# Sigmoid attention with a squared-ReLU feed-forward layer: another order of products in 48 units, and other idle products at the start

## The chip, the core and the metric

The kernel runs on one core of a Trainium2 chip. The metric is the device time of one execution in microseconds (us). A core has five engines with queues of their own: TensorE (PE, with its weight loads shown apart as PEld) multiplies, VectorE (DVE) and ScalarE (ACT) work element by element, GpSimd (POOL) does nearly nothing here, and SyncE (SP) issues the transfers.

## What is computed

The first part is an attention whose softmax is replaced by a sigmoid, over 8 batches of 12 heads, 448 positions and 64 numbers a head. Its result, 3584 tokens of 768 numbers, goes through a feed-forward layer with a hidden width of 2048:

```python
scores = q @ k.T / sqrt(64) - log(448)
x = sigmoid(scores) @ v              # 3584 tokens x 768
h = x @ w_in                         # 768 -> 2048
g = s * relu(h) ** 2 + b
out = g @ w_out                      # 2048 -> 768
```

All inputs and outputs are float32.

## The kernel before

**Attention (lines 352 to 406).** A loop goes over 24 groups of four heads. For each group `scores` and `scores_last` make the scores with float32 products over half the rows (64 of 128 partitions), two at a time; ScalarE takes the sigmoid of each pair of banks (line 354), `attn_v` and `attn_v_last` multiply by v, and the result goes to memory. The tiles of the sigmoids have eight buffers (the pool `ap_`, tag "a"). In the same steps VectorE and ScalarE convert the weights, which come as 64-bit numbers, and form sums of blocks of them (the planner of lines 416 to 469), which are stored for later.

**The start.** The first group's queries and keys are loaded in two halves, `load(..., first=True)`, lines 344 and 345: k, q, k, q. Meanwhile TensorE runs `WARM` = 17 idle products of a tile of zeros in bfloat16 (lines 410 to 412), 256 columns each, into a PSUM tile `idle` that nobody reads. Then come the scores of the first group: six pairs for the first half of the queries, and six for the second.

**Feed-forward layer.** Each float32 matrix is split into a high part, rounded to float32r, and a low part, the rest. A product of two matrices is made of three: high x high, high x low and low x high (`PARTS`, line 37: index of the weights' part, index of the tokens' part). The first 512 tokens are computed plainly: line 487 (`ffn1`) puts 18 products into one bank, line 666 (`ffn2`) three into each of six banks. The other six blocks of 512 tokens are computed three at a time, in two rounds (`n` = 0 and 1), with a scheme that takes 15 block products instead of 18, for either layer.

**The units of the first layer.** A round has 60 units, 15 block products `i` by four parts `p` of the hidden width, in the order of `L1` (line 554), which is written out by hand in `CHAINS_1`: the block products of a chain go to the same PSUM tile `bk`, of two banks, and the parts of a pair (0, 1) or (2, 3) take turns. A unit is twelve products of 128x128 weights with 512 columns: for each of its two banks `j`, two blocks `c` of the inner dimension, and for each the three of `PARTS`. So its first six products go to bank 0 and the next six to bank 1, and the second product of each three has the same weights as the first (line 922, inside three loops):

```python
for j in range(2):
    m = 0
    for c in range(KC):
        for wi, xi in PARTS:
            nc.tensor.matmul(bk[:, j], wt[:, j, wi, c * P : (c + 1) * P], opd[i][xi][:, c, :], ...)
```

After each unit `results_1` (lines 795 to 838) copies or adds `bk`, both banks in one instruction, into tiles in SBUF on ScalarE or VectorE; `square` and `scale` follow. The weights `wt` of a unit come by one transfer of 512 KB into one of seven buffers, which the SP queue issues six units ahead (`fetch`). Other jobs for the operands of later units (`first_jobs`) are placed in the units by hand (`places`). The second layer, line 1049, has 60 units of twelve products as well, each half of which adds to a bank.

Of the kernel before, what the change touches and what calls it, by code (L numbers as in the profile page):

```python
# [12 lines left out]
F32R = mybir.dt.float32r  # L13
# [4 lines left out]
AF = mybir.ActivationFunctionType  # L18
# [16 lines left out]


TB = 512
WARM = 17
PARTS = ((0, 0), (0, 1), (1, 0))
AHEAD = 6  # L40
PIECES = (2, 1, 1, 2, 1, 1, 2, 1, 1, 2, 1, 1, 2, 1, 1, 2, 1, 1, 2, 1, 2, 1)
# [43 lines left out]
def sigmoid_attention_relu2_ffn(  # L85
# [11 lines left out]
    nc = tc.nc  # L97
    B, NQ, P, _, S = q.shape
    D = v.shape[5]
    NF, _, DM = w_in.shape  # L100
# [4 lines left out]
    KC = NCC // 3  # L105
# [8 lines left out]
    def pool(stack, name, bufs, side=None, space=None):  # L114
        kw = dict(side=side) if side else {}
        if space is not None:
            kw["space"] = space
        return stack.enter_context(
            tc.tile_pool(name=name, bufs=bufs, reuse_waits="tile", **kw)
        )  # L120
# [22 lines left out]
    first = ExitStack()  # L143
# [11 lines left out]
    zero = const.tile([P, 2 * P], BF16, name="zero")  # L155
# [170 lines left out]
    ap_ = pool(at, "ap", 8)  # L326
# [7 lines left out]
    half = (slice(0, D), slice(D, P))  # L334
# [22 lines left out]
    def scores(b, t, i, ld_):  # L357
        qt, kt, _ = ld_
        a = []
        for c in range(3):  # L360

            pl, tag = (ps_av, "pav") if i == 0 and c == 2 else (ps_qk, "psc")
            psc = pl.tile([P, 2, 512], F32, tag=tag, name=f"psc_{b}_{t}_{i}_{c}")
            for j, r in enumerate(half):
                nc.tensor.matmul(  # L365
                    psc[:, j, :S], kt[r, i, c * P : (c + 1) * P], qt[r, i, :],
                    start=True, stop=True,
                )
            a.append(sigmoid(psc, f"{b}_{t}_{i}_{c}"))
        return a  # L370
# [39 lines left out]
    idle = ps_qk.tile([P, 2, 512], F32, tag="psc", name="idle")  # L410
    for _ in range(WARM):
        nc.tensor.matmul(idle[:, 0, : 2 * P], zero[:, :P], zero, start=True, stop=True)

    plan = {}
# [100 lines left out]
    for n, (b, t) in enumerate(quads):  # L517
        ticks(n, "DVE")
        a = [scores(b, t, i, loaded[n]) for i in range(2)]
# [52 lines left out]
    def load_raw(n, m, k):  # L572
        A[m, k] = slot(f"a_{n}_{m}{k}")
        load_tokens(A[m, k], threes[n][m], KC * k, KC)
# [22 lines left out]
    opd = {}  # L597
# [78 lines left out]
    start = [(0, 0), (2, 0), (2, 1), (2, 2), (0, 2), (0, 1), (1, 1), (1, 2), (1, 0)]  # L676
# [4 lines left out]
    for i, f in enumerate(order):  # L681
# [17 lines left out]
        j, stage = divmod(i - LATE_AT, LATE_FOR)  # L699
# [37 lines left out]
    def out_store(src, e, t, n):  # L737
        dst = out[e * P : (e + n) * P, t * TB : (t + 1) * TB]
        nc.sync.dma_start(dst.rearrange("(c p) t -> p c t", p=P), src)
# [25 lines left out]
    def weights():  # L765
        fetch()
        return fetched[next(pos_)]
# [7 lines left out]
    }  # L775
    LAST = ((0, slice(0, TB)), (1, slice(0, TB // 2)), (1, slice(TB // 2, TB)))
    LEAD = 3

    for n, blocks in enumerate(threes):

        G = {}
        banks = {}
# [4 lines left out]
        def results_1(i, p, bk):  # L787


            def g(m, h):  # L790
                return G[m, h, p]

            def copy(m, h):
                G[m, h, p] = slot(f"G_{n}_{m}{h}{p}")
                nc.scalar.copy(g(m, h), bk)  # L795

            def final(m, h, neg=False):
                x = g(m, h)
                if (m, h) == (0, 0):
                    scales.append(lambda: (act_square(x), scale(x)))  # L800
                else:
                    later.append(lambda: (square(x, neg), scales.append(lambda: scale(x))))

            if i == 4:
                copy(0, 0)
            elif i == 3:
                copy(2, 0)
            elif i == 10:
                copy(2, 1)
            elif i == 13:  # L810
                add(g(2, 0), g(2, 0), bk)
            elif i == 2:
                copy(0, 1)
            elif i == 1:
                add(g(0, 1), g(0, 1), bk)
                x, y = g(0, 0), g(0, 1)
                later.append(lambda: (add(x, x, y), final(0, 0)))
            elif i == 8:
                sub(g(0, 1), bk, g(0, 1))
            elif i == 12:  # L820
                copy(1, 0)
            elif i == 7:
                add(g(2, 0), g(2, 0), bk)
                final(2, 0, True)
            elif i == 9:
                add(g(2, 1), g(2, 1), bk)
            elif i == 11:
                sub(g(1, 0), bk, g(1, 0))
                copy(1, 1)
                final(1, 0)  # L830
            elif i == 5:
                sub(g(1, 1), bk, g(1, 1))
            elif i == 0:
                sub(g(0, 1), g(0, 1), bk)
                final(0, 1)
            elif i == 6:
                sub(g(1, 1), g(1, 1), bk)
                final(1, 1)
            else:
                add(g(2, 1), g(2, 1), bk)  # L840
                final(2, 1)
# [65 lines left out]
        for u, (i, p) in enumerate(L1):  # L907
            wt = weights()
            if n == 0 and u < 4:
                load_raw(0, *start[5 + u])  # L910
            if outs and u > 4:
                out_store(outs[0], evict[6 - 2 * len(outs)], 0, 2)
                heap.free(outs.pop(0))
            ch = next(c for c in CHAINS_1 if i in c)
            if i == ch[0]:
                banks[p] = ps.tile([P, 2, TB], F32, tag="b", name=f"h_{n}_{i}_{p}")
            bk = banks[p]
            for j in range(2):
                m = 0
                for c in range(KC):  # L920
                    for wi, xi in PARTS:
                        nc.tensor.matmul(  # L922
                            bk[:, j], wt[:, j, wi, c * P : (c + 1) * P], opd[i][xi][:, c, :],
                            start=i == ch[0] and m == 0,
                            stop=m == 3 * KC - 1,
                            skip_group_check=True,
                        )
                        m += 1
            if p == NPP - 1:
                for t in opd.pop(i):  # L930
                    heap.free(t)
                for key in {3: ("3",), 13: ("13",), 2: ("2",), 9: ("9",), 5: ("10",), 0: ((0, 2),),
                            12: ((1, 1),), 11: ((1, 2),), 14: ((2, 0),)}.get(i, ()):
                    A.pop(key)
            here = places.get(u, ())
            casts = []
            for q_ in (10,) * (n == 0 and u < 2) + here:
                fn = todo[q_].pop(0)
                if u < 4 and fn.__name__ == "hi":
                    casts.append(fn)  # L940
                else:
                    fn()
            if u >= len(L1) - LEAD:
                prep(u - len(L1) + LEAD)
            ready, scales = scales, []
            for _ in range(2 - len(here)):
                if later:
                    later.popleft()()
            results_1(i, p, bk)
            for fn in casts + ready:  # L950
                fn()
# [82 lines left out]
        for j, (i, p) in enumerate(L2):  # L1034
            wt = weights()
            ch = next(c for c in CHAINS_2 if i in c)
            if i == ch[0] and p == 0:
                banks[ch] = ps.tile([P, 2, TB], F32, tag="b", name=f"o_{n}_{i}")
            bk = banks[ch]
            g = gc.pop(j)  # L1040
            end = n + 1 == len(threes) and j + 1 == len(L2)

            for e, tk in LAST if end else [(e, slice(TB)) for e in range(KC)]:
                o = bk[:, e]
                if end:
                    o = ps.tile([P, 2, TB], F32, tag="b", name=f"o_{e}_{tk.start}")[:, 0, tk]
                for f in range(2):
                    for m, (wi, gi) in enumerate(PARTS):
                        nc.tensor.matmul(  # L1049
                            o, wt[:, f, wi, e * P : (e + 1) * P], g[gi][:, f, tk],  # L1050
                            start=(end or i == ch[0] and p == 0) and f == 0 and m == 0,
                            stop=p == NPP - 1 and f == 1 and m == 2,
                            skip_group_check=True,
                        )
                if end:
                    x = C["t"][:, e, tk]
# [9 lines left out]
            if j in loads:  # L1066
                load_raw(n + 1, *loads[j])
            prep(j + LEAD)
            if later:
# [45 lines left out]
```

## Time and profile before

| | |
|---|---|
| median of three runs | 1059.9 us (1059.56 to 1059.91) |
| profiled execution | 1060.09 us |
| its span, first to last instruction | 1057.9 us |
| TensorE busy | 1053.0 us (100%), 5015 products |
| weight loads | 756.2 us (71%), 5015 loads |
| VectorE busy | 794.0 us (75%) |
| ScalarE busy | 585.7 us (55%) |
| transfers | 280.84 MB, 265 GB/s |

How to read the profile: the page has each engine's busy time, the chain of work that ended last (followed back from the last instruction to what released it), and groups of instructions by line, each with its count, total busy time and mean duration. Products are pipelined: a product of 512 columns is listed with 389 ns from its start to its modelled end, while the next one starts 227 ns after it. So what a product costs is read from starts, or from the chain, where a row gives the start, the time on the chain and the number of products. Rows of a timeline merge neighbours that are alike: "x2" with 0.61 us is two products, the second starting 0.22 us after the first.

### The profile page before, as it was taken

The page shows a single profiled execution, that of the slowest core. Times are in us where ns is not written, and L with a number is a line of the kernel's source. Part 1 is how long each engine was busy: PE and PEld are TensorE (multiplying, and loading weights), DVE is VectorE, ACT ScalarE, POOL GpSimd, SP SyncE. Part 2 cuts the span into 40 slices and gives each one's busy share as a digit, 9 for nine tenths or more (in the row PEclk, how much of TensorE's full clock was granted, in tenths as well). Part 3 has the DMA queues.
Part 4 walks back from the last instruction along what each step waited for, and adds up shares of the span by engine and source line. Part 5 has one row for each costly group of instructions (what it writes and reads, how often), then busy time and mean ns, then how long its engine had stood idle before and what let it go on. Part 6 is the DMA issues. An engine that isn't in the chain of part 4 may idle for free.

```text
span 1057.9 us, 13349 instructions
## 1 busy us (share of the span) xinstructions
PE 1053.0 (100%) x5015; PEld 756.2 (71%) x5015; DVE 794.0 (75%) x915; ACT 585.7 (55%) x638; POOL 0.2 (0%) x4
## 2 busy tenths in 40 slices
PE   9999999999999999999999999999999999999998
PEld 4443433333788888888888888888888888888887
DVE  3777877778788876455888799597445789888777
ACT  6777777778776765354436443344444336443432
POOL 0000000000000000000000000000000000000000
PEclk9999999999999999999999999999999999999999
DMA  8899999997899999866666677797666666667673
GB/s 300 280 338 372 332 330 336 340 371 295 323 380 344 374 356 407 289 196 197 187 194 197 194 234 230 250 335 272 197 196 188 195 197 193 189 229 224 206 234 117
DMA packets 105470, 280.84 MB, mean 265 GB/s; under 512 B 10560, under 2 KB 26688, under 8 KB 105408
## 3 DMA queue, kind: packets, MB, share of 16 engines
q1 hardware_dynamic: 105408, 280.01, 77.8%
q8 instruction: 40, 0.66, 0.2%
q14 instruction: 22, 0.18, 0.0%
HBM read 195.04 MB, written 84.93 MB: 265 GB/s over the span
## 4 chain that ended last, share of the span: by engine, by line
PE 99%; DMA 1%; SPq 0%; DVE 0%; issue 0%
PE o L1049 31%; PE h L922 31%; PE pav L388 11%; PE psc L365 11%; PE ph L487 6%; PE po L666 6%; PE pav L397 2%; PE psc_l L377 2%; DMA q<-q_t 1%; SPq L344 0%; SPq L345 0%; DVE C_t L174 0%
## 5 line engine op out<-in xcount | busy, mean ns | idle before, releaser
L922 PE MATMUL h<-s_1h,wu 128*128 128x512 f32 x480 | 148.0, 389 | 0.0
L922 PE MATMUL h<-s_0h,wu 128*128 128x512 f32 x480 | 147.8, 389 | 0.0
L354 ACT ACTIVATE a<-psc,nls 128x896 f32<-128x896 f32 x144 | 132.1, 1018 | 3.7 <-PE psc L365 3.7
L365 PE MATMUL psc<-q,k 64*128 64x448 f32 x576 | 115.5, 546 | 0.6 <-DMA q<-q_t 0.6
L388 PE MATMUL pav<-a,v 128*64 128x448 f32 x576 | 113.5, 543 | 0.0
L922 PEld LDWEIGHTS h<-s_1h,wu 128*128 128x128 f32 x480 | 90.1, 188 | 18.8
L922 PEld LDWEIGHTS h<-s_0h,wu 128*128 128x128 f32 x480 | 90.1, 188 | 18.6
L795 ACT COPY G<-h 128x1024 f32<-128x1024 f32 x48 | 48.9, 1018 | 92.7 <-PE h L922 60.9
L365 PEld LDWEIGHTS psc<-q,k 64*128 64x128 f32 x576 | 53.3, 186 | 61.9 <-issue 37.1
L171 DVE TENSOR_TENSOR G<-G,h 128x1024 f32<-128x1024 f32 x40 | 48.8, 1220 | 61.1 <-PE h L922 61.1
L761 ACT ACTIVATE G<-G,b_sb,s_sb 128x1024 f32<-128x1024 f32 x48 | 59.8, 1246 | 62.8 <-DVE G L758 62.1
L922 PE MATMUL h<-s_0l,wu 128*128 128x512 f32 x240 | 93.4, 389 | 0.0
L922 PE MATMUL h<-s_1l,wu 128*128 128x512 f32 x240 | 93.4, 389 | 0.0
L388 PEld LDWEIGHTS pav<-a,v 128*64 128x64 f32 x576 | 39.2, 137 | 71.4 <-issue 63.6
L1049 PE MATMUL o<-g_3h,wu 128*128 128x512 f32 (+1 forms) x244 | 79.0, 385 | 0.0
L1049 PE MATMUL o<-g_0h,wu 128*128 128x512 f32 x240 | 78.8, 389 | 0.0
L1049 PE MATMUL o<-g_1h,wu 128*128 128x512 f32 x240 | 78.8, 389 | 0.0
L1049 PE MATMUL o<-g_2h,wu 128*128 128x512 f32 x240 | 78.8, 389 | 0.0
L405 DVE COPY xo<-pav 128x448 f32<-128x448 f32 x48 | 27.7, 620 | 55.3 <-PE pav L397 55.3
L666 PE MATMUL po<-g,w 128*128 128x512 f32 x288 | 67.7, 389 | 0.0
L666 PEld LDWEIGHTS po<-g,w 128*128 128x128 f32 x288 | 54.1, 188 | 11.2
L487 PE MATMUL ph<-x0h,w 128*128 128x512 f32 x192 | 61.7, 390 | 0.0
(126 smaller groups left out, 1823.4 us busy)
## 6 DMA issues: line engine op xcount, KB each, us to landing
wu<-wd SPq DMA_DIRECT2D x240, 512.0 KB, 3.5
wd<-t SPq DMA_DIRECT2D x48, 768.0 KB, 8.9
st<-w_out SPq DMA_DIRECT2D x16, 768.0 KB, 8.4
st<-w_in SPq DMA_DIRECT2D x16, 768.0 KB, 8.7
wd<-w SPq DMA_DIRECT2D x16, 768.0 KB, 5.3
v<-v_t SPq DMA_DIRECT2D x24, 448.0 KB, 6.3
xd<-xo SPq DMA_DIRECT2D x48, 224.0 KB, 6.5
k<-k_t SPq DMA_DIRECT2D x23, 448.0 KB, 4.1
```

The costliest lines, as they stand in the source:

```text
L171: nc.vector.tensor_tensor(o, x, y, op=ALU.add)
L354: nc.scalar.activation(a, psc[:, :, :S], AF.Sigmoid, bias=nls, scale=SCALE)
L365: nc.tensor.matmul(psc[:, j, :S], kt[r, i, c * P : (c + 1) * P], qt[r, i, :], start=True, stop=True,)
L377: nc.tensor.matmul(psc[half[i], j, :S], kt[r, i, 3 * P :], qt[r, i, :], start=True, stop=True,)
L388: nc.tensor.matmul(pav[r, i, :S], ld_[2][:, 3 * i + c, j, :], a[i][c][:, j, :], start=c == 0, stop=False,)
L405: nc.vector.tensor_copy(o, pav[:, i, :S])
L487: nc.tensor.matmul(ph, w[:, k, wi, kc * P : (kc + 1) * P], x0[h][xi][:, cc, :], start=m == 0, stop=m == 3 * NCC - 1,)
L666: nc.tensor.matmul(pos[e], w[:, k, wi, kc * P : (kc + 1) * P], g[:, gi, :], start=first and i == 0, stop=last and i == 2,)
L761: nc.scalar.activation(x, x, AF.Identity, bias=b_sb, scale=s_sb)
L795: nc.scalar.copy(g(m, h), bk)
L922: nc.tensor.matmul(bk[:, j], wt[:, j, wi, c * P : (c + 1) * P], opd[i][xi][:, c, :], start=i == ch[0] and m == 0, stop=m == 3 * KC - 1, sk ...
L1049: nc.tensor.matmul(o, wt[:, f, wi, e * P : (e + 1) * P], g[gi][:, f, tk], start=(end or i == ch[0] and p == 0) and f == 0 and m == 0, stop ...
```

## The change

In the round `n` = 0 units 8 to 31 ("banks") make their twelve products with the two banks taken in turn: product by product, first bank 0, then bank 1. Units 32 to 55 ("parts") keep the order of banks and take the three products of each block as high x high, low x high, high x low (weights' part first), so that no weights come twice in a row. The other units, and the whole round `n` = 1, are as before. The same products are computed everywhere. At the start, 8 idle products in bfloat16 are left of 17; a new tile `zr` of float32r zeros is written by three ScalarE copies from `zero`, and 8 idle products in float32r of 448 columns follow: two over all 128 rows, then six over half the rows, the upper and the lower half in turn, into the two banks of `idle`.

```diff
-WARM = 17
+WARM = 8
...
     for _ in range(WARM):
         nc.tensor.matmul(idle[:, 0, : 2 * P], zero[:, :P], zero, start=True, stop=True)
+
+    zr = ap_.tile([P, 2, S], F32R, tag="a", name="zr")
+    nc.scalar.activation(zr[:, 0, : 2 * P], zero, AF.Copy)
+    nc.scalar.activation(zr[:, 1, : 2 * P], zero, AF.Copy)
+    nc.scalar.activation(zr[:, 1, 2 * P :], zero[:, : S - 2 * P], AF.Copy)
+    for x in range(2):
+        for _ in range((1, 3)[x]):
+            for j, r in enumerate(half):
+                r = r if x else slice(P)
+                nc.tensor.matmul(
+                    idle[:, j, :S], zr[r, 0, :P], zr[r, 1, :S], start=True, stop=True
+                )
...
+    ORDERS = {
+        "banks": range(8, 32), "parts": range(32, 56)
+    }
...
             bk = banks[p]
-            for j in range(2):
-                m = 0
-                for c in range(KC):
-                    for wi, xi in PARTS:
-                        nc.tensor.matmul(
+            new = i == ch[0]
+            kind = next((x for x, us in ORDERS.items() if u in us), "") if n == 0 else ""
+
+            def product(o, w, x, first, last):
+                nc.tensor.matmul(
+                    o, w, x, start=first, stop=last,
+                    skip_group_check=True,
+                )
+
+            if kind == "banks":
+                for m, (c, (wi, xi)) in enumerate((c, y) for c in range(KC) for y in PARTS):
+                    for j in range(2):
+                        product(
                             bk[:, j], wt[:, j, wi, c * P : (c + 1) * P], opd[i][xi][:, c, :],
-                            start=i == ch[0] and m == 0,
-                            stop=m == 3 * KC - 1,
-                            skip_group_check=True,
+                            new and m == 0, m == 3 * KC - 1,
                         )
-                        m += 1
+            else:
+                parts = ((0, 0), (1, 0), (0, 1)) if kind == "parts" else PARTS
+                for j in range(2):
+                    for m, (c, (wi, xi)) in enumerate((c, y) for c in range(KC) for y in parts):
+                        product(
+                            bk[:, j], wt[:, j, wi, c * P : (c + 1) * P], opd[i][xi][:, c, :],
+                            new and m == 0, m == 3 * KC - 1,
+                        )
```

## Rows read from the trace of the kernel before

**Rows 1.** The page: span, busy times, and the chain that ended last.

```profile
span 1057.9 us, 13349 instructions
PE 1053.0 (100%) x5015; PEld 756.2 (71%) x5015; DVE 794.0 (75%) x915; ACT 585.7 (55%) x638; POOL 0.2 (0%) x4
...
PE 99%; DMA 1%; SPq 0%; DVE 0%; issue 0%
PE o L1049 31%; PE h L922 31%; PE pav L388 11%; PE psc L365 11%; PE ph L487 6%; PE po L666 6%; PE pav L397 2%; PE psc_l L377 2%; DMA q<-q_t 1%; SPq L344 0%; SPq L345 0%; DVE C_t L174 0%
```

**Rows 2.** TensorE's waits: for whom, us in total, times, longest us.

```profile
PE idle L412 <- DVE nls L157: 1.0, 1, 1.0
PE psc L365 <- DMA q<-q_t: 0.6, 1, 0.6
```

**Rows 3.** The chain in order of time: start us, us, what.

```profile
2.11 5.43 DMA q<-q_t
7.54 0.14 issue
7.68 2.53 PE psc L365 x12
...
381.40 4.08 PE ph L487 x18
385.48 4.08 PE po L666 x18
...
401.80 163.20 PE h L922 x720
```

**Rows 4.** Windows of both groups: span, busy us (count) by engine, clock, DMA.

```profile
423.56:488.84 65.28, 65.28 (x290) 54.05 (x289) 34.67 (x29) 31.42 (x31) 0.00 (x0) 1.00 0.73 234
488.84:554.12 65.28, 65.28 (x290) 54.05 (x289) 50.12 (x42) 24.48 (x22) 0.00 (x0) 1.00 0.65 193
```

**Rows 5.** Line 922's weight loads: count, ns min/median/max, first and last start.

```profile
L922 PEld LDWEIGHTS h<-s_0h,wu x480: 187/188/188, 401.4 to 564.4; 128*128 128x128 f32 x160
...
L922 PEld LDWEIGHTS h<-s_0l,wu x240: 187/188/188, 401.6 to 564.2; 128*128 128x128 f32 x120
```

**Rows 6.** Timeline of TensorE in line 922: start us, us, what.

```profile
423.63 0.39 PE L922 MATMUL h<-s_0l,wu 128*128 128x512 f32 x1
423.86 0.61 PE L922 MATMUL h<-s_0h,wu 128*128 128x512 f32 x2
...
429.75 0.39 PE L922 MATMUL h<-s_0l,wu 128*128 128x512 f32 x1
429.98 0.39 PE L922 MATMUL h<-s_0h,wu 128*128 128x512 f32 x1
```

**Rows 7.** Groups of the page: readers of a unit's banks.

```profile
L795 ACT COPY G<-h 128x1024 f32<-128x1024 f32 x48 | 48.9, 1018 | 92.7 <-PE h L922 60.9
L171 DVE TENSOR_TENSOR G<-G,h 128x1024 f32<-128x1024 f32 x40 | 48.8, 1220 | 61.1 <-PE h L922 61.1
```

**Rows 8.** Timeline of TensorE at the start: start us, us, what.

```profile
1.05 3.60 PE L412 MATMUL idle<-zero 128*128 128x256 bf16 x17 [1.05 <-DVE nls L157]
4.57 2.53 PE L365 MATMUL psc<-q,k 64*128 64x448 f32 x12
7.68 2.53 PE L365 MATMUL psc<-q,k 64*128 64x448 f32 x12 [0.58 <-DMA q<-q_t]
```

**Rows 9.** The idle products: ns min/median/max, first and last start.

```profile
L412 PE MATMUL idle<-zero x17: 273/421/421, 1.0 to 4.4; 128*128 128x256 bf16 x17
```

**Rows 10.** Window of the start, columns as in rows 4.

```profile
3.00:3.50 0.50, 0.50 (x4) 0.38 (x3) 0.00 (x0) 0.00 (x0) 0.00 (x0) 1.00 1.02 351
```

**Rows 11.** Timeline of the first scores' weight loads: start us, us, what.

```profile
5.05 0.19 PEld L365 LDWEIGHTS psc<-q,k 64*128 64x128 f32 x2 [0.18 <-issue]
5.43 0.19 PEld L365 LDWEIGHTS psc<-q,k 64*128 64x128 f32 x2 [0.18 <-issue]
5.81 0.19 PEld L365 LDWEIGHTS psc<-q,k 64*128 64x128 f32 x2 [0.18 <-issue]
```

**Rows 12.** Timeline of ScalarE at the start: start us, us, what.

```profile
2.02 0.20 ACT L158 ACTIVATE e_bias<-nls 128x1 f32<-128x1 f32 x1
5.64 2.80 ACT L354 ACTIVATE a<-psc,nls 128x896 f32<-128x896 f32 x3 [3.42 <-PE psc L365]
```

**Rows 13.** Groups of ScalarE by shape: count, busy us, mean ns, idle before.

```profile
L354 ACT ACTIVATE a<-psc,nls 128x896 f32<-128x896 f32 x144 | 132.1, 1018 | 3.7 <-PE psc L365 3.7
...
L282 ACT CAST td<-td 128x512 fp32r<-128x512 f32 x8 | 4.9, 617 | 0.6 <-DVE td L171 0.6
L158 ACT ACTIVATE e_bias<-nls 128x1 f32<-128x1 f32 x1 | 0.2, 205 | 0.0
```

## The prediction

> **What bounds the kernel now.** I read the page's busy times and its chain first: TensorE is busy for 1053.0 of 1057.9 us, and the chain that ended last is 99% products, of them 31% on line 922 [rows 1]. Second, the waits of TensorE: two in the whole execution, 1.0 us for the zeros of the idle products and 0.6 us for the first queries [rows 2]. So from 7.68 us on, a stage costs what its products cost one after another, and whatever another engine saves is worth nothing. Third, the chain in order of time [rows 3]. The reader is to see in it that 720 products of line 922 take 163.20 us, so 226.67 ns each, and that 18 products of line 487 and 18 of line 666 take 4.08 us, the same 226.67 ns. Ahead of 7.68 us stands the transfer of the second half of q, 5.43 us, and not TensorE. The profiled execution took 1060.09 us: its span and 2.2 us around it. The median of the three runs is 1059.9, so a sum made against the profile is lowered by 0.2 us at the end.
>
> **The change has two parts.** One sets the order of the twelve products in 48 of the 60 units of the first block of line 922; the other replaces 9 of 17 idle products at the start by 8 others, fed by three new ScalarE copies. No transfer is added or moved, so SP's queue is as before.
>
> **Part 1a, banks in turn (units 8 to 31 of the first block).** Number of products: as before, 24 x 12 = 288, in the stretch 423.56 to 488.84 us [rows 4]. What is new is that each product goes to the other bank than the one before. A unit now changes bank twice in twelve products (once within, once to the next unit); it will change twelve times, 10 more, 240 in the 24 units. The price of a change of bank can be bounded from the rows of before: line 487 puts 18 products into one bank, line 666 puts three into each of six banks, and both take 4.08 us [rows 3]. The readings are rounded to 0.01 us, and line 666 has five changes more, so a change costs between -2 and +2 ns. 240 x 2 ns gives -0.5 to +0.5 us. I take 0: the 720 products of line 922, with a change at every sixth, have that mean too.
>
> **Part 1b, no weights twice running (both groups of 24 units).** Today four of a unit's twelve products have the weights of the one before (high part of the weights with high, then with low part of the tokens). The first group loses these four too, since its two banks belong to two halves of the weights. So 48 x 4 = 192 repetitions go. Is a repetition cheaper now? There is one weight load for every product, 5015 and 5015 [rows 1], and the loads ahead of high and of low parts take 187 to 188 ns alike [rows 5]: nothing is skipped, so nothing is lost. The starts say the same. From a low product to the next, where the weights change, ten steps (the first and the last shown) are 0.23 us six times and 0.22 four times, mean 0.226; the mean over all is 0.2267 [rows 6]. With the rounding I put a repetition within 3 ns of a change, 192 x 3 ns = -0.6 to +0.6 us, and take 0.
>
> **What waits could come from the new order.** The results of a unit are read by one instruction over both banks (128x1024, 1.02 us on ScalarE, 1.22 on VectorE [rows 7]), so a unit's first product waits for that reader in either order; the second bank being written 0.23 instead of 1.36 us into the unit adds no wait. Cover: another unit of 12 x 0.2267 = 2.72 us lies between two units of one bank pair, and VectorE and ScalarE are busy 34.67 and 31.42 us of 65.28 in the one stretch, 50.12 and 24.48 in the other [rows 4]. If that cover went, each unit would stall for the excess. The low part of the tokens is needed by the third product, not the second: 0.23 us more room. Weight tiles come free with a unit's last product as before.
>
> **Part 2, the start.** Removed: 9 idle products of 256 columns. 17 from 1.05 us take 3.60 us [rows 8], most of them 421 ns and the shortest 273 [rows 9], so they start (3.60 - 0.27)/16 = 0.21 us apart. That is 1.2 columns per ns, the 1.2 GHz level, although the windows view writes a granted clock of 1.00 there too [rows 10]. One product is down to 273 ns, and the first scores, from 4.57 us, go a pair each 0.376 us by their weight loads [rows 11], so six pairs of either half end 2.53 us after they begin [rows 8]. So I read the clock as up by about 4.5 us. Now step by step:
> - 8 idle products: 1.05 + 7 x 0.21 + 0.42 = 2.94 us.
> - Three ScalarE copies (256, 256 and 192 columns) follow e_bias, which ends at 2.02 + 0.20 = 2.22 us [rows 12]. 1 column takes 0.20 us, 512 columns 0.62 [rows 13]; between them 256 are 0.41 and 192 are 0.36 us (my interpolation). One after another 1.18 us; overlapped as the sigmoids are (three in 2.80 us [rows 12], where one takes 1.02 [rows 13]: 0.13 less each), 0.9 us. So the zeros are ready at 3.15 to 3.40 us. ScalarE was idle for 3.42 us there and has its next work at 5.64: free on ScalarE. TensorE, queued behind, has a new wait of 0.2 to 0.45 us.
> - Two full idle products of 448 columns: at the low level 448/1.2 = 0.373 us each, to 4.15 us.
> - Six over half the rows. No row shows float32r over half the rows. The float32 scores over half the rows are loaded in pairs [rows 11]; if these go two at a time too, at the column rate of line 922, three pairs take 0.37 each at the low level and 0.2 at the high one: ready between 4.9 and 5.3 us. If one after another at the low level, 6 x 0.373: 6.4 us. I take the pairs, 5.0 us.
> - Then six pairs of scores, 6 x 0.376 = 2.26 us, before the second half can start, which waited for q until 7.68 [rows 3, 8]. Slack: 7.68 - 4.57 - 2.26 = 0.85 us. A start at 4.9 to 5.3 lies within it: cost 0. A start at 6.4 us costs 1.0 us. Nothing can be gained, since q lands when it lands.
> - The buffer that the zeros take is one of eight of the sigmoid tiles, free again before the first of them comes round: 0.
>
> **Sum:** 1060.1 + 0 + 0 + 0 us on the profile's scale, 1059.9 on the median's. I write 1060.0, a little of the start's wait counted in. What a measurement of this kernel can tell from no change is 0.2%, 2.1 us.
>
> **Rivals.**
> - *Alternating banks are dearer.* Only single changes of bank are in the trace, never one at each product. A product takes 226.67 ns, where 512 columns at the high level (twice the pace of the idle products) are 213.3; what the other 13.3 ns are, no row tells. If alternation doubled them, 288 x 13.3 ns = 3.8 us: 1063.7. It decides from 7.4 ns a product (2.1 us / 288). Against it: lines 487, 666 and 922 with one, six and two banks at the same pace. Chance 0.05.
> - *The new order is cheaper,* the 13.3 ns being a price of the old one: 576 x 13.3 ns = 7.7 us, 1052.2. Against it the same rows. Chance 0.03.
> - *The clock rises later,* because the idle stretch now has a hole from about 2.94 to 3.3 us. Each pair of scores at the low level would take about 0.75 us instead of 0.376. From 5.3 us all six of the first half at the low level end at 9.8 us, 2.1 us after 7.68. So a rise within that half costs 0 to 2.1 us, 1059.9 to 1062.0; half rows that go one after another give 1.0 us in the same bracket. For it: the rise in the trace came after a stretch without a hole. Against it: the hole is short. Chance 0.22. If the clock stays low through the second half too, 2.26 us more: up to 1064.3, slower. Chance 0.03.
> - *Taking banks in turn makes the clock fall.* As a mechanism here: the 65.28 us of units 8 to 31 at the low level, 288 x 426.7 ns = 122.9 us, 57.6 more: 1117.5. Against it: the stage of lines 487 and 666, whose products go through six banks, keeps 226.67 ns, and the granted clock reads 1.00 in every stretch. Chance 0.01.
>
> The Trainium skill, "TensorE: Matmul & The Clock Gate", section "A second HAM failure mode: psum-queue depth-cycling", tells of a kernel with 512-column products that cycled through PSUM banks, paused between groups and had its clock go up and down; by that rule the last rival would hold. The trace disagrees so far as it goes: line 666 cycles and has no pauses. The same page, "Part 1: The HAM clock gate", says that the slow state is the default and that sustained activity releases it; by it the hole at the start speaks for the third rival, and the trace shows only a rise without one.
>
> **How the numbers follow.** Forecast 0.66 (1059.9, with the bounds of parts 1a and 1b 1058.8 to 1061.0); a later rise within the first half 0.22; the four others 0.12. Faster by over 0.2%: 0.03. Slower by over 0.2%: 0.05 + 0.03 + 0.01 = 0.09. Same: 0.88. The bounds of 1a and 1b seldom add up at their ends, so the range is 1059.1 to 1062.0: it holds nearly all of the forecast and of the later rise, and leaves out the 0.12.
>
> **What would show it.** In the chain of the changed kernel, 720 products of line 922 (whatever its new line) again in 163.20 us, and steps of 0.22 or 0.23 us between starts in both groups; a step of 0.21 or 0.24 makes parts 1a or 1b wrong. In the timeline of the start: a wait of TensorE for ScalarE's copies of 0.2 to 0.45 us, the half-row products two at a time, the first scores by 5.3 us, the second half of the scores at 7.7 us behind q. The last item is the one that counts: if the second half starts later, the delay is the change's cost, and the duration of the first scores tells whether the clock or serial half rows made it.

## Result and profile after

The changed kernel takes 1061.17 us (median of 20 runs, 1060.60 to 1062.15) against 1059.91 us before (20 runs, 1059.22 to 1060.58). The ratio is 1.0013, interval 1.0007 to 1.0019: slower by 1.26 us (1.33 by the means), within the 0.2% that were called "no change", but beyond what the interval leaves to chance. The profiled execution took 1060.60 us, the shortest of the 20; its span is 0.5 us longer than that of before. Two slow executions of the kernel before, of 1530.44 and 3821.01 us, which stand beside runs of the next section, count in no ratio and no difference of means.

The page of the changed kernel: span, busy times, and the chain that ended last, by engine.

```profile
span 1058.4 us, 13350 instructions
PE 1053.9 (100%) x5014; PEld 756.5 (71%) x5014; DVE 794.1 (75%) x915; ACT 587.0 (55%) x641; POOL 0.2 (0%) x4
...
PE 99%; ACT 1%; DVE 0%; issue 0%
```

The chain in order of time (start us, us, what), which answers to [rows 3].

```profile
2.84 0.26 ACT zr L417
3.10 0.04 issue
3.14 2.53 PE idle L422 x7
5.67 1.17 PE psc L365 x4
6.85 0.02 issue
6.87 3.72 ACT a L354 x4
10.59 0.04 issue
10.63 0.98 PE psc_l L377 x8
...
402.31 163.20 PE h L938 x720
```

Two things are to be seen. The 720 products of the first round, 576 of them in a new order, take 163.20 us as before. And they begin at 402.31 instead of 401.80 us: the whole 0.5 us of this execution arises before them. The chain no longer begins with the transfer of q; it runs through ScalarE's copies, the idle products, four scores and four sigmoids.

TensorE in both groups of units, by its timeline: units in turn of banks first (low x 2, high x 4), then units with no weights twice running. It answers to [rows 6].

```profile
429.80 0.62 PE L938 MATMUL h<-s_0l,wu 128*128 128x512 f32 x2
430.25 1.07 PE L938 MATMUL h<-s_0h,wu 128*128 128x512 f32 x4
431.16 0.62 PE L938 MATMUL h<-s_0l,wu 128*128 128x512 f32 x2
...
499.84 0.39 PE L938 MATMUL h<-s_0l,wu 128*128 128x512 f32 x1
500.06 0.62 PE L938 MATMUL h<-s_0h,wu 128*128 128x512 f32 x2
500.52 0.39 PE L938 MATMUL h<-s_0l,wu 128*128 128x512 f32 x1
```

Six products from 429.80 to 431.16 are 0.227 us each, three from 499.84 to 500.52 are 0.227 us each: the pace of before in both.

The start, by TensorE's timeline, answering to [rows 8], and the timeline of the weight loads, answering to [rows 11].

```profile
1.05 1.89 PE L412 MATMUL idle<-zero 128*128 128x256 bf16 x8 [1.05 <-DVE nls L157]
3.14 2.53 PE L422 MATMUL idle<-zr 128*128 128x448 f32 x8 [0.20 <-ACT zr L417]
5.47 5.10 PE L365 MATMUL psc<-q,k 64*128 64x448 f32 x24
```

```profile
3.14 0.50 PEld L422 LDWEIGHTS idle<-zr 128*128 128x128 f32 x2 [0.69 <-ACT zr L417]
4.18 0.87 PEld L422 LDWEIGHTS idle<-zr 64*128 64x128 f32 x6 [0.55 <-issue]
5.10 0.70 PEld L365 LDWEIGHTS psc<-q,k 64*128 64x128 f32 x4
6.22 0.25 PEld L365 LDWEIGHTS psc<-q,k 64*128 64x128 f32 x2 [0.41 <-issue]
6.66 0.19 PEld L365 LDWEIGHTS psc<-q,k 64*128 64x128 f32 x2 [0.19 <-issue]
7.03 0.19 PEld L365 LDWEIGHTS psc<-q,k 64*128 64x128 f32 x2 [0.19 <-issue]
...
8.16 0.19 PEld L365 LDWEIGHTS psc<-q,k 64*128 64x128 f32 x2 [0.19 <-issue]
```

There is the hole of 0.20 us (end to start) for ScalarE's copies; the float32r products from 3.14 us; the first scores at 5.47 instead of 4.57 us; and the pace. From 6.66 on the pairs of scores follow each other in 0.37 us, 0.44 before that, and the first pair, whose products start at 5.47, took about 0.74: the clock was at its lower level until 6.2 to 6.7 us, where before the first scores already had the high one. The traces bear this out directly. Each holds a record of the granted clock, which begins with the rise to 2.4 GHz, and the views write 1.00 for the time ahead of it. The rise stands at 4.29 us in the trace of before and at 6.33 us in this one.

The weights of a pair are loaded while the pair before it runs, so the load at 8.16 us marks the start of the seventh pair, the first of the second half. That is 0.48 us later than the 7.68 us of before [rows 8], nearly all of the 0.51 us by which line 922 begins later.

### The profile page after: what moved, and what is told of

It reads as the page before. It is cut to its first block, busy times and chain, and to the rows that moved or that the text cites. A ratio compares the mean times of both kernels' runs of the same rounds, so it can differ in the third digit from the quotient of the medians.

```text
span 1058.4 us, 13350 instructions
## 1 busy us (share of the span) xinstructions
PE 1053.9 (100%) x5014; PEld 756.5 (71%) x5014; DVE 794.1 (75%) x915; ACT 587.0 (55%) x641; POOL 0.2 (0%) x4
## 4 chain that ended last, share of the span: by engine, by line
PE 99%; ACT 1%; DVE 0%; issue 0%
PE o L1078 31%; PE h L938 31%; PE pav L388 11%; PE psc L365 10%; PE ph L499 6%; PE po L678 6%; PE pav L397 2%; PE psc_l L377 2%; ACT a L354 0%; PE idle L422 0%; ACT L158 0%; DVE C_t L174 0%; ACT zr L415 0%; ACT zr L416 0%; ACT zr L417 0%; ACT e_bias L158 0%
## 5 line engine op out<-in xcount | busy, mean ns | idle before, releaser
L938 PE MATMUL h<-s_0h,wu 128*128 128x512 f32 x480 | 140.1, 389 | 0.0
L938 PE MATMUL h<-s_0l,wu 128*128 128x512 f32 x240 | 85.6, 389 | 0.0
```

The source lines that it names most:

```text
L938: nc.tensor.matmul(o, w, x, start=first, stop=last, skip_group_check=True,)
```

## The experiments

All were timed beside the kernel before on the same chip, 11 executions each (before 15 to 33). "Before" is the median there, "difference" that of the means, which the ratio follows too. The medians of eleven are not steady enough for differences of some tenths: hole_small, for one, has seven executions between 1059.64 and 1060.05 us and four between 1060.73 and 1061.02. "Hole" is the wait of TensorE, from end to start, after the first idle products (orders_only also waits 0.21 us ahead of the scores, when the clock is already up). "Clock up" is the rise in the trace's record of the granted clock, "fast pace" the time from which the pairs of scores follow each other in 0.38 us in the one profiled execution, "line 922" the start of its 720 products in that execution's chain. They took 163.20 us in every one of them.

| kernel | us | before | difference, us | ratio, interval | hole, us | clock up, us | fast pace, us | line 922, us |
|---|---|---|---|---|---|---|---|---|
| orders_only | 1059.68 | 1060.24 | -0.15 | 0.9999 (0.9990 to 1.0008) | none | 4.01 | 4.7 | 401.19 |
| banks_all | 1059.62 | 1060.24 | -0.26 | 0.9997 (0.9988 to 1.0006) | none | 6.82 | 7.0 | 402.17 |
| start_only | 1061.21 | 1060.24 | +1.22 | 1.0012 (1.0003 to 1.0021) | 0.20 | 7.61 | 7.7 | 402.80 |
| after_again | 1061.28 | 1060.24 | +1.28 | 1.0013 (1.0004 to 1.0022) | 0.20 | 8.15 | 8.3 | 403.08 |
| hole_filled | 1060.25 | 1060.21 | +0.18 | 1.0002 (0.9993 to 1.0011) | none | 5.84 | 6.0 | 402.06 |
| hole_small | 1060.02 | 1060.11 | +0.31 | 1.0003 (0.9994 to 1.0012) | none | 4.48 | 4.8 | 401.64 |
| full_warm | 1060.96 | 1060.21 | +0.90 | 1.0009 (1.0000 to 1.0018) | none | 4.55 | 5.8 | 402.68 |
| eight_alone | 1060.90 | 1060.21 | +0.82 | 1.0009 (1.0000 to 1.0018) | 1.06 | 9.59 | 9.9 | 403.12 |
| bf16_after_hole | 1060.42 | 1060.21 | +0.24 | 1.0002 (0.9993 to 1.0011) | none | 5.03 | 5.4 | 402.02 |
| bf16_equal_hole | 1060.66 | 1060.11 | +0.45 | 1.0003 (0.9994 to 1.0012) | 0.20 | 6.76 | 6.8 | 402.43 |
| bf16_late_end | 1060.25 | 1060.03 | +0.27 | 1.0002 (0.9993 to 1.0011) | 0.20 | 6.38 | 6.4 | 402.43 |
| bf16_wide_hole | 1061.53 | 1060.11 | +1.36 | 1.0012 (1.0003 to 1.0021) | 1.06 | 7.76 | 8.0 | 402.83 |

### Which part of the change costs

**orders_only**: the change without its start.

```diff
-WARM = 8
+WARM = 17
-    zr = ap_.tile([P, 2, S], F32R, tag="a", name="zr")
...
-                nc.tensor.matmul(
-                    idle[:, j, :S], zr[r, 0, :P], zr[r, 1, :S], start=True, stop=True
-                )
```

> The start of before (17 bfloat16 idle products, no float32r zeros) with both new orders in the 48 units. Theory S (all of the 1.26 us between the medians comes from the start): the time of before within 0.3 us, and the first round of line 922's products in 163.20 us. Rival O (the orders cost something in executions other than the one profiled): 0.7 us or more above before, at least the part of the 1.26 us that the two profiled spans (1058.4 against 1057.9) do not show.

**start_only**: the change without its orders.

```diff
-        "banks": range(8, 32), "parts": range(32, 56)
+        "banks": (), "parts": ()
```

> The new start with the old order in every unit. Theory S: 1.0 to 1.5 us above before, as the changed kernel is, with the scores' sigmoids beginning at 6.5 us or later instead of 5.64. Rival O: 0.5 us above before, what the two profiled spans show, and the rest missing.

**banks_all**: as orders_only, and banks in turn in all 120 units.

```diff
-        "banks": range(8, 32), "parts": range(32, 56)
+        "banks": range(60), "parts": ()
-            kind = next((x for x, us in ORDERS.items() if u in us), "") if n == 0 else ""
+            kind = next((x for x, us in ORDERS.items() if u in us), "")
```

> The start of before, and the two banks taken in turn in all 120 units of the first layer, 1440 products instead of 288. Theory S: the time of before within 0.3 us. Rival O: five times what the 24 units cost; a price of 2 ns for each product, the bound taken from the rows of before, would be 2.9 us. If the order were cheaper by the 13.3 ns between 226.67 and 213.3, 19 us less.

**after_again**: the changed kernel, unedited.

> The changed kernel once more, for a second trace of its start. Theory S with the clock as its cause: the pair of first scores from which their pace turns from about 0.74 to 0.38 us is another one than in the first trace, and the span moves with it, by about 0.37 us for each pair. A rival within S (only the length of the new idle stretch counts): the first scores begin at 5.5 us and go at the same pace as in the first trace, and the span is 1058.4 again, within 0.2 us.

By the means the orders alone are 0.15 us below before and the 1440 alternating products 0.26 us below, both with intervals around 1; the start alone is 1.22 us above (its sigmoids begin at 7.21 us), the whole change 1.28 us. Theory S holds and O falls (by the medians, 0.56 and 0.62 us below, S would have missed its 0.3 us, but on the faster side). By banks_all's interval, a change of bank costs between -1.1 and +0.5 ns (-0.0012 and +0.0006 of 1060 us, over 1200 changes more, ten in each of 120 units). The chain says it more closely. Here are the two rounds of line 922 (here 925) in banks_all, which alternate throughout:

```profile
402.17 163.20 PE h L925 x720
...
728.57 163.20 PE h L925 x720
```

Each has 600 changes more than the same round of before and takes the same 163.20 us, so with the rounding to 0.01 us a change costs less than 0.02 ns.

After_again's weight loads show the clock at its lower level for longer than in the first trace:

```profile
6.22 0.34 PEld L365 LDWEIGHTS psc<-q,k 64*128 64x128 f32 x2 [0.41 <-issue]
6.96 0.34 PEld L365 LDWEIGHTS psc<-q,k 64*128 64x128 f32 x2 [0.41 <-issue]
7.71 0.34 PEld L365 LDWEIGHTS psc<-q,k 64*128 64x128 f32 x2 [0.41 <-issue]
8.31 0.19 PEld L365 LDWEIGHTS psc<-q,k 64*128 64x128 f32 x2 [0.27 <-issue]
8.69 0.19 PEld L365 LDWEIGHTS psc<-q,k 64*128 64x128 f32 x2 [0.19 <-PE psc L365]
9.06 0.19 PEld L365 LDWEIGHTS psc<-q,k 64*128 64x128 f32 x2 [0.19 <-issue]
```

Pairs 0.75 us apart up to 7.71, and 0.38 from 8.31. Three traces have the same start (first scores at 5.47) and differ in the clock alone: fast pace at 6.7, 7.7 and 8.3 us, line 922 at 402.31, 402.80 and 403.08. Each us by which the pace turns later costs about half a us, as a pair at half the pace must. In the same three traces the second half of the scores begins at 8.16, 8.79 and 9.06 us, 0.48, 1.11 and 1.38 us later than before, and line 922 0.51, 1.00 and 1.28 us later: the delay of the scores' second half is the change's cost. The rival in which only the length of the idle stretch counts falls: the spans were 1058.4, 1058.9 and 1059.2.

### The hole

**hole_filled** has 10 bfloat16 products ahead of the float32r ones instead of 8, **hole_small** 9, **full_warm** 17; the rest is the changed kernel.

```diff
-WARM = 8
+WARM = 10
```

> The changed kernel with 10 bfloat16 idle products instead of 8, so that TensorE has work until the float32r zeros are there and the idle stretch ends at the same 5.5 us. Theory H (the hole delays the rise of the clock): the scores' pace turns to 0.38 us a pair between 4.2 and 7.1 us, as in the three traces with 17 idle products, and the time is 1060.0 to 1060.6. Rival F (float32r products over few or half the rows do not bring the clock up, or only the later end of the idle stretch counts): the pace turns at 6.5 us or later and the time stays at 1061.0 to 1061.5.

> The changed kernel with nine bfloat16 idle products instead of eight: 0.2 us less of the hole, the float32r products and their gaps as they are, and the same end of the stretch. Theory H with a price that grows with the hole: between 1060.3 and 1061.0. If a hole that the timeline no longer shows costs nothing: 1060.0 to 1060.5, as with ten products. Rival G with the float32r gaps as the main part: 1061.0 or more.

> The changed kernel with 17 bfloat16 idle products ahead of the eight in float32r: no hole, and the longest idle stretch. Theory H: the clock is up before the first scores in most executions, so that these go at 0.38 us a pair throughout; they begin at 5.8 to 7.0 us, and the time is 1060.3 to 1061.0, by the length alone. Rival F: the pace turns within the scores, at 7 us or later, and the time is above 1061.3.

TensorE's timelines of hole_filled (first three rows) and hole_small have no wait for the copies. The idle stretch ends at the time of the changed kernel in hole_filled, and earlier in hole_small, where the clock rose within it:

```profile
1.05 2.31 PE L412 MATMUL idle<-zero 128*128 128x256 bf16 x10 [1.05 <-DVE nls L157]
3.14 2.53 PE L422 MATMUL idle<-zr 128*128 128x448 f32 x8
5.47 4.85 PE L365 MATMUL psc<-q,k 64*128 64x448 f32 x24
...
1.05 2.10 PE L412 MATMUL idle<-zero 128*128 128x256 bf16 x9 [1.05 <-DVE nls L157]
3.14 2.06 PE L422 MATMUL idle<-zr 128*128 128x448 f32 x8
5.04 4.99 PE L365 MATMUL psc<-q,k 64*128 64x448 f32 x24
```

By the means they are 0.18 and 0.31 us above before (by the medians 0.04 above and 0.09 below). All 22 executions of the two lie between 1059.49 and 1061.02, their mean is 1060.26; the 42 with the new start as it is (the result's 20, start_only and after_again) lie between 1060.60 and 1062.15, their mean is 1061.27; the means of before beside them are 1059.94 to 1060.05. The float32r products and their gaps are in both sets: one or two more idle products, which close the hole, take away about 1.0 of the 1.3 us. Rival F falls for them, and so does G with the float32r gaps as the main part. H holds. By its median hole_small fits the form in which a hole that the timeline no longer shows costs nothing; its mean of 1060.29 lies between that and a small price. From start to start it still has 0.41 us there, where 0.21 is the pace. In full_warm the clock is up before the first scores, which begin at 5.82 us, and its time is in the range that was expected. That the length alone makes its 0.90 us is not shown: in the one trace the second half of the scores waits until 8.55 us for q, which landed at 8.41 us, and that is the whole delay of this execution.

**eight_alone** has no float32r products, so that TensorE waits for q after 2.94 us.

```diff
-    zr = ap_.tile([P, 2, S], F32R, tag="a", name="zr")
...
-                nc.tensor.matmul(
-                    idle[:, j, :S], zr[r, 0, :P], zr[r, 1, :S], start=True, stop=True
-                )
```

**bf16_after_hole** puts nine bfloat16 products in their place.

```diff
-    zr = ap_.tile([P, 2, S], F32R, tag="a", name="zr")
+    zr = ap_.tile([P, 2, S], BF16, tag="a", name="zr")
...
+    for _ in range(9):
+        nc.tensor.matmul(
+            idle[:, 0, : 2 * P], zr[:, 0, :P], zr[:, 1, : 2 * P], start=True, stop=True
+        )
```

> Eight bfloat16 idle products and nothing else, with the new orders: TensorE has nothing from 2.95 us until the first half of q is there at about 4.1 us. Theory H: the scores begin half a microsecond earlier than before, but at 0.75 us a pair until 7.5 us or later, and the time is 1060.6 to 1061.6. Rival F: with no float32r products and no later end of the idle stretch, the time is that of before within 0.3 us, or below it.

> The changed kernel with the zeros copied into a bfloat16 tile and nine bfloat16 products of 256 columns in place of the eight in float32r: the hole stays, the float32r products go, the idle stretch ends at about 5.1 us. Theory H: the pace turns at 6.5 us or later, the time is 1060.7 to 1061.4. Rival F: the pace turns between 4.2 and 7.1 us, the time is within 0.3 us of before.

Eight_alone, by the timelines of TensorE and of its weight loads:

```profile
3.99 7.54 PE L365 MATMUL psc<-q,k 64*128 64x448 f32 x24 [1.06 <-DMA q<-q_t]
```

```profile
6.37 0.37 PEld L365 LDWEIGHTS psc<-q,k 64*128 64x128 f32 x2 [0.38 <-issue]
7.11 0.37 PEld L365 LDWEIGHTS psc<-q,k 64*128 64x128 f32 x2 [0.38 <-issue]
...
9.85 0.20 PEld L365 LDWEIGHTS psc<-q,k 64*128 64x128 f32 x2 [0.17 <-issue]
10.23 0.20 PEld L365 LDWEIGHTS psc<-q,k 64*128 64x128 f32 x2 [0.17 <-issue]
```

The scores begin 0.6 us earlier than before and still end later: the clock rises at 9.59 us, and the first 16 of the 24 products start at the lower level. This is as theory H said, with a hole of 1.06 us; but here the products behind the hole are gone as well. Bf16_after_hole gave what F said, but its edit did not do what was meant: the new products read only what the first two copies write, so they began at 2.88 us and left no hole, as its timeline shows.

```profile
1.05 1.89 PE L412 MATMUL idle<-zero 128*128 128x256 bf16 x8 [1.05 <-DVE nls L157]
2.88 2.08 PE L419 MATMUL idle<-zr 128*128 128x256 bf16 x9
```

It belongs to the kernels without a hole. **bf16_equal_hole** mends it: the products wait for all three copies. **bf16_late_end** has ten and a half of them, so that the stretch ends as in the changed kernel; **bf16_wide_hole** is bf16_equal_hole with `WARM = 4`.

```diff
-            idle[:, 0, : 2 * P], zr[:, 0, :P], zr[:, 1, : 2 * P], start=True, stop=True
+            idle[:, 0, : 2 * P], zr[:, 0, :P], zr[:, 1, S - 2 * P : S], start=True, stop=True
```

Bf16_late_end against bf16_equal_hole:

```diff
-    for _ in range(9):
+    for w in (2,) * 10 + (1,):
         nc.tensor.matmul(
-            idle[:, 0, : 2 * P], zr[:, 0, :P], zr[:, 1, S - 2 * P : S], start=True, stop=True
+            idle[:, 0, : w * P], zr[:, 0, :P], zr[:, 1, S - w * P : S], start=True, stop=True
         )
```

> Eight bfloat16 idle products, then nine bfloat16 ones that wait for all three copies, so that the hole is as long as in the changed kernel (about 0.2 us between the ends and the starts that the timeline shows, 0.6 from start to start), with no float32r product. Theory H (the hole alone delays the clock): the pace of the scores turns at 6.5 us or later, the time is 1060.7 to 1061.4. Rival G (the hole and the gaps between the first float32r products, 0.5 us from start to start, delay it together): the time is within 0.4 us of before.

> Eight bfloat16 idle products, the hole of the changed kernel, and ten and a half bfloat16 products instead of nine, so that the stretch ends as late as in the changed kernel (first scores at 5.47 us instead of 5.14), still with no float32r product. If the later end is what the changed kernel has on top of the hole (1061.2 against 1060.66): 1061.0 to 1061.4. By the pace alone a start 0.33 us later costs half of that while the clock is low: 1060.7 to 1060.9, and the rest of the changed kernel's cost would lie with the float32r products behind the hole.

> The same with four products ahead of the hole instead of eight, so that the hole is 0.85 us longer and the stretch ends at the same time. Theory H, and G as well if only the length of all gaps counts: 1060.7 to 1061.4, the pace turning at 6.5 us or later. If the clock's rise is not tied to holes of this kind at all: within 0.4 us of before.

By the means, the same hole with bfloat16 behind it costs 0.45 and 0.27 us, no more than can be told from the 0.18 to 0.31 us of the kernels without a hole, and less than the 1.22 to 1.33 us with float32r behind it. The intervals are about 1 us to either side, so single kernels are hard to tell apart; the 22 executions of these two have a mean of 1060.34 us against 1061.27 for the 42. The wide hole, whose timeline follows, costs 1.36 us (1061.53 by the median, a little above the 1061.4 of its forecast):

```profile
1.05 1.03 PE L412 MATMUL idle<-zero 128*128 128x256 bf16 x4 [1.05 <-DVE nls L157]
3.13 2.08 PE L419 MATMUL idle<-zr 128*128 128x256 bf16 x9 [1.06 <-ACT zr L417]
```

So a hole of 1.06 us is enough to delay the clock. That the hole of 0.20 us alone makes the whole cost is not shown; theory H in that form said 1060.7 to 1061.4 for bf16_equal_hole, which took 1060.66, and bf16_late_end is below both of its forecasts. So the later end does not explain the rest either. What is shown is that the two together cost: the hole of 0.20 us with float32r products behind it 1.2 to 1.3 us, the hole with bfloat16 behind it and the float32r products without a hole 0.2 to 0.5 us each. That is nearest to rival G, in which the hole and the gaps between the first float32r products delay the clock together. What stays open is why.

The recorded clock agrees, with one trace of each kernel: in the seven traces with a hole it rises at 6.33 to 9.59 us, in the seven without, before among them, at 4.01 to 5.84 us and once, in banks_all, at 6.82. The two sets meet there, and the moment is a matter of the execution too. Another thing no run separates: in hole_filled and hole_small the hole is closed by more products, so whether the pause counts or the work that is missing in it is not told. Bf16_after_hole and bf16_equal_hole have the same 17 idle products without and with the hole, but there the costs are too close, 0.24 and 0.45 us.

## Why the prediction was right or wrong

**What bounds the kernel**: right. In every trace the products of line 922 keep 163.20 us, and what differs arises before them.

**Parts 1a and 1b**: right, at 0. The bounds, 2 ns for a change of bank and 3 ns for a repetition, were wide enough: the rounds of the same 163.20 us leave less than 0.02 ns for a change and about 0.05 ns for each of the 192 repetitions that are gone. The rivals of a dearer and of a cheaper order (0.05 and 0.03) fall: neither the bank nor the repetition has to do with the 13.3 ns. So does the clock falling by turns of banks: banks_all alternates in every product of 326 us and keeps its pace. The section that the prediction cites for this rival, "A second HAM failure mode: psum-queue depth-cycling" of the Trainium skill's "TensorE: Matmul & The Clock Gate", is about a kernel that idles briefly between groups. Here banks_all cycles without pauses and loses nothing. That the granted clock "reads 1.00 in every stretch" was no evidence for the start, where the views write 1.00 ahead of the first record; behind it, the record has no fall before the last product ends.

**Part 2, the pieces**: the eight products ended at 2.94 us, as worked out. The copies took 0.40, 0.40 and 0.35 us and were ready at 3.10, just under the 3.15 to 3.40. The hole was 0.20 us, the low end of 0.2 to 0.45. The half-row products go two at a time, as I took it: six from 4.18 to 5.47 us, 1.3 us instead of 2.24. The two full ones took 1.04 us instead of 0.75, and the first scores began at 5.47, not 5.0 and outside the 4.9 to 5.3.

**Part 2, the step that failed**: "So I read the clock as up by about 4.5 us", carried over to a stretch that had a hole, and with it "A start at 4.9 to 5.3 lies within it: cost 0". The reading was right for the trace of before (4.29 us); in the three traces of the new start the clock rose at 6.33, 7.61 and 8.15 us. The six pairs of the first half then took 2.69, 3.32 and 3.59 us instead of the 2.26 of the sum. The third rival, that the clock rises later within the first half, got 0.22 and 0 to 2.1 us; 1.26 us lies well inside. It came true, with the clock as its mechanism, and it should have been the forecast: its argument for (the only rise in the trace came after a stretch without a hole) was a row, the one against it ("the hole is short") was none. That the hole by itself does it, as the rival had it, is shown for 1.06 us and not for 0.20. The Trainium skill, "TensorE: Matmul & The Clock Gate", "Part 1: The HAM clock gate", says that the lower clock is the default and that activity has to release it. That agrees with hole_small, hole_filled and bf16_wide_hole.

**The slack** of 0.85 us was nearly the right size: of the 0.48 us by which the second half began later in the first trace of after, the start at 5.47 instead of 4.57 us makes 0.05, and the slower pace 0.43. This is the sign that the prediction called the one that counts, and it points to the clock and not to serial half rows. But the slack was counted on TensorE and q alone. In the first trace of after the 24 scores end at 10.57 us (5.47 + 5.10), and the products behind them start at 10.63, when the fourth sigmoid frees a PSUM buffer: the sigmoids, which began at 6.87 instead of 5.64 us, are the chain from 6.87 to 10.59. They end only just after TensorE, so this adds little here; but behind q both TensorE's row of scores and ScalarE's of sigmoids can come to bind, and the prediction named neither. Nor does q come at a fixed time: in this trace the 24 scores ran without a wait for it, and in orders_only as well, whose line 922 begins 0.61 us earlier than that of before.

**The numbers**: 1061.17 lies in the range of 1059.1 to 1062.0, and "same" by 0.2% was right; the median expected, 1060.0, was 1.2 us low. The forecast proper went to 1061.0 at most, with both bounds of part 1 at their ends, and these turned out to be nothing. So the range holds the result only because it was drawn to take in the third rival, and "same" only because 0.2%, 2.1 us, is as wide as that rival's whole bracket.

## What to carry to other kernels

Let idle products that warm up TensorE follow each other without a hole: if some of them wait for operands of another kind, put enough of the first kind ahead to cover the time until these are there. Here, ahead of float32r products, one product of 0.21 us decided over about 1 us; ahead of bfloat16 products a hole of 0.20 us showed no such price. When a start shifts, follow every engine of the first stage to where its work is next awaited, the eviction of PSUM too, before calling a shift free; and do not take the moment of a clock's rise from one trace as a property of the kernel. Where differences are a thousandth, read lists of executions and means, not a median of eleven.

## What was not expected of the hardware

- With the same 17 idle products and no hole, the fast pace came at 4.6 us in the trace of before, 4.7 in that of orders_only and 7.0 in that of banks_all. The record of the clock has the rise at 4.29, 4.01 and 6.82 us. The moment varies between executions, and with it the time, though a wait for q can hide part of it: line 922 of banks_all begins 0.98 us after that of orders_only, but only 0.37 after that of before, which waited for q. The second half of q varies too: orders_only ran all 24 scores without a wait for it, while in full_warm it was there at 8.41 us. The first two rows below are from the chain of orders_only, the third is from that of full_warm.

```profile
4.72 4.78 PE psc L365 x24
...
401.19 163.20 PE h L925 x720
```

```profile
2.10 6.31 DMA q<-q_t
```

- The first float32r products after bfloat16 ones take more than their columns: two of 448 columns 1.04 us at the lower level, where 0.75 would do (weight loads at 3.14 and 4.18 us above). In the steady stream of line 922 nothing of the kind is seen.
- Products over half the rows in float32r, upper and lower half in turn, run two at a time, as the float32 scores do.
